# A gated delta-rule attention with a softplus MLP on one core: the first pair of chunks inverted chunk by chunk, and a new order of all items

## The chip, the cores and the metric

The kernel runs on one core of one Trainium2 chip, as one program. Time is device microseconds (us) of that core; three runs of the kernel before gave 239.97, 241.2 and 242.23, median 241.2. A profile of one further execution goes with it.

## The reference

Four batches of eight heads, 768 time steps, head size 48. A linear-attention state of 48 by 48 per head is read and updated at each step, and the gated result goes through an MLP with softplus (3072 tokens, 384 to 2048 to 384):

```python
k_n = k / (np.linalg.norm(k, axis=-1, keepdims=True) + 1e-06)
for t in range(S):
    kt, vt, bt = (k_n[:, :, t].copy(), v[:, :, t].copy(), beta[:, :, t, None].copy())
    readout = np.einsum('bhd,bhde->bhe', q[:, :, t], state)
    y[:, :, t] = g[:, :, t] * readout
    v_old = np.einsum('bhde,bhd->bhe', state, kt)
    state = state + bt[:, :, :, None] * np.einsum('bhd,bhe->bhde', kt, vt - v_old)
...
x = np.ascontiguousarray(attn_out.transpose(0, 2, 1, 3)).reshape(B * S, H * D)
h = x @ w_in
g = np.maximum(h, 0.0) + np.log1p(np.exp(-np.abs(h)))
return (g @ w_out).astype(np.float32)
```

## The kernel before, in words

**Chunks.** The 768 steps are cut into 12 chunks of 64. Within a chunk the recurrence is solved at once: with G the products of the chunk's keys with each other, the effect of the steps on each other is the inverse of a 64 by 64 lower triangular matrix for each of 32 heads. Only the state then passes from chunk to chunk. Each chunk goes through four kinds of work.

- *Loads and norms* (`norms`, `front`): k, q, v and g of a chunk come in as two DMAs of 192 KB each, all issued by SyncE (SP) but for a few. The keys are squared (`ksq`, L348 to L350), summed over 48 (`red`, L359), and the root is taken (`sqrt` on ScalarE, ACT, for chunks 0 to 3, `pow` on GpSimd, POOL, after that) with `eps` behind it. Keys and queries are cast or scaled to fp16 (`cast`, `kmul`), transposed on TensorE (PE; `trs`, L419 and L451) and copied out of PSUM (`kev`, `qev`).
- *Products* (`gram`, L513): keys with keys, and keys with queries. The first are copied out negated (`kkc`, into the tile kk), the second are masked by VectorE, DVE (`mask`, L495). For chunks 0 and 1 (`N_SPLIT = 2`) both are separate items of 64 columns; later chunks have one item of 128. For chunks 0 and 1 there is also `gramd` (L537), which gives the 32 by 32 diagonal blocks alone, copied out as `kd`.
- *Inverse* (`inverse`), for a pair of chunks at a time (`GROUPS`): the 16 by 16 diagonal blocks are brought into lanes by a DVE transpose (`ln`, L594 or L601), scaled by beta (`prep`, L641), and inverted by 15 steps that depend on each other (`step`, L653 to L668; step j is a product into tmp and a sum into tt of 2(15-j)(j+1) elements, on DVE or POOL). The result is masked into three buffers (`ca`, `cb`, L683 and L685) and transposed back (`st`, L711, three for a pair). Two rounds of small matmuls (`xmm` L741, `tmm` L771, then `zmm` L792, with `xs`, `td2` and `z` copying out of PSUM) build the 64 by 64 inverse from its blocks.
- *Chain* (`chain`), one chunk after the other: `ks` and `qs` (L829) apply the old state, `w` (L869) subtracts, `umm` (L883) and `zu` (L896) apply the inverse with copies `u1` and `u2`, `smm` (L913) and `s` (L927) make the new state, `ymm` (L939), `y` (L953), `ytr` (L966) and `xt` give the chunk's gated output, transposed. For chunk 0 there is no old state, and `w0` (L861) scales v.
- *Dense*: `g1` (L992, six matmuls of 256 columns or three of 512 twice), softplus on ACT (`soft`, L1004), `g2` (L1019, four matmuls of 384 columns) and `o`, then a store. Chunks 0, 1, 10 and 11 have dense jobs of their own (16 items of g1 and g2 each), 2 to 9 go in pairs (32 items). The weights come in eight quarters by DMAs that POOL issues (`wload`, L327).

**Order.** Nothing is scheduled by rule: `emit` runs one table (`_ORDER`) of some 1260 words such as `D227`, an engine's letter (P, D, A, G for POOL, S for SyncE) and an item's number. So each engine's queue has one fixed order, and an instruction that waits holds back all behind it on its engine. `fill` items (L1049) are matmuls on the identity whose result nobody reads; the table has twelve of them, four matmuls each.

**beta for chunks 0 and 1** comes by four DMAs that POOL issues ahead of its first work (L179), into lanes laid out for the pair; the rest of beta by eight DMAs on SP (L262).

Of the kernel before, what the change touches and what calls it, by code (L numbers as in the profile page):

```python
# [87 lines left out]
def kernel(  # L88
# [474 lines left out]

    def inverse(gi):
# [8 lines left out]
        if RAW[c0]:  # L573
            nl, bl, nv = Buf(r_nl), Buf(r_bl), nv_of[c0]

            def lbeta(en):
                nc.vector.transpose(nl.ap, nv.ap)
                nc.vector.reciprocal(nl.ap, nl.ap)
                nc.vector.tensor_tensor(bl.ap, beta_l[:, gi], nl.ap, ALU.mult)
                nc.vector.tensor_tensor(bl.ap, bl.ap, nl.ap, ALU.mult)  # L580

            bl_it = [add("lbeta", tag, "D", lbeta, deps=[nv_it[c] for c in cs], bufs=[nv, nl, bl])]
            blb, bl_of = [bl], lambda: bl.ap
        else:
            bl_it, blb, bl_of = [], [], lambda: beta_l[:, gi]
# [4 lines left out]
        def lnt(en):  # L590
            o = words(ln.ap.rearrange("p w s e -> p (w s e)"))[:, : nw * HC]
            if compact:
                i = words(kd_of[gi].ap.rearrange("p c u t -> p (c u t)"))
                nc.vector.transpose(  # L594
                    o.rearrange("p (w n) -> p w n", w=nw),
                    i.rearrange("p (n w) -> p w n", w=nw),
                )
                return
# [132 lines left out]
        def uv(ap):  # L731
            return ap.rearrange("p (u c) -> p u c", c=HC)

        for cl, c in enumerate(cs):
            xp, ep, xs = [Buf(p_d), Buf(p_d)], [Buf(p_d), Buf(p_d)], Buf(r_xs)

            def xmm(en, cl=cl, xp=xp):
                for n in range(H):
                    for p in range(2):
                        for r in range(2):  # L740
                            nc.tensor.matmul(  # L741
                                uv(xp[p].ap)[HALF[r ^ p], n],
                                kk.ap[HALF[r], cl, H * p + n, HC:],
                                dn.ap[HALF[r], cl, H * p + n],
                            )

            e3 = add("xmm", f"{c}", "P", xmm, deps=[ta_it] + kk_it[c], bufs=[kk, dn] + xp, mm=32,
                     mode="64")
            def pickx(en, xp, xs, p):
                o = xs.ap[:, H * p : H * p + H].rearrange("p u (x b j) -> p u x b j", x=2, b=2)  # L750
                i = uv(xp[p].ap)[:, :H].rearrange("p u (x j) -> p u x j", x=2)
                if en == "D":
                    nc.vector.tensor_tensor(
                        o[:, :, :, 0], i, mk[:, None, :, None].broadcast_to([P, H, 2, 16]),
                        ALU.mult)
                    return
                for x in range(2):
                    nc.scalar.activation(
                        o[:, :, x, 0], i[:, :, x], AF.Copy, scale=mk[:, x : x + 1])

            e4 = [add("xs", f"{c}.{p}", "DA",
                      lambda en, xp=xp, xs=xs, p=p: pickx(en, xp, xs, p),
                      deps=[e3], bufs=[xp[p], xs], size=256)
                  for p in range(2)]

            def tmm(en, cl=cl, ep=ep, xs=xs):
                for n in range(H):
                    for p in range(2):
                        for r in range(2):
                            h = HALF[r ^ p]  # L770
                            nc.tensor.matmul(  # L771
                                uv(ep[p].ap)[HALF[r], n],
                                xs.ap[h, H * p + n],
                                tx.ap[h, cl, n] if p else tb.ap[h, cl, n],
                            )

            e5 = add("tmm", f"{c}", "P", tmm, deps=e4 + [tb_it] + tx_it, bufs=[xs, tb, tx] + ep,
                     mm=32, mode="64")
            td2 = [add("td2", f"{c}.{p}", "AD",
                       lambda en, cl=cl, ep=ep, p=p: copy(  # L780
                           en,
                           td.ap[:, cl, H * p : H * p + H]
                           .rearrange("p u (k b j) -> p u k b j", k=3, b=2)[:, :, 1:, 1],
                           uv(ep[p].ap)[:, :H].rearrange("p u (x j) -> p u x j", x=2)),
                       deps=[e5], bufs=[ep[p], td], size=256)
                   for p in range(2)]
            zp, z = [Buf(p_d), Buf(p_d)], Buf(r_z)

            def zmm(en, cl=cl, zp=zp):
                for r, p, i, m in CROSS:  # L790
                    u = H * p + 2 * i + m
                    nc.tensor.matmul(  # L792
                        zp[r].ap.rearrange("p (n c) -> p n c", c=64)[HALF[r ^ p], 2 * i + m, :HC],
                        kk.ap[HALF[r], cl, u, : 2 * HC],
                        td.ap[HALF[r], cl, u, 2 * HC :],
                    )

            z1 = add("zmm", f"{c}", "P", zmm, deps=td2 + [td_it], bufs=[kk, td] + zp, mm=32,
                     mode="64")
            z_it = []  # L800
            for r in range(2):
                z_it.append(
                    add("z", f"{c}.{r}", "AD",
                        lambda en, r=r, z=z, zp=zp: copy(
                            en, z.ap[:, r, :, HC:],
                            zp[r].ap.rearrange("p (n c) -> p n c", c=64)[:, :, :HC]),
                        deps=[z1], bufs=[zp[r], z], size=256))
            td_of[c] = td
            z_of[c] = (z, z_it, [td_it] + td2)
# [356 lines left out]
```

## Time and profile before

| | |
|---|---|
| runs | 239.97, 241.2, 242.23 us |
| profiled execution | 240.57 us, of which the span of its instructions is 238.9 us |
| busy | PE 217.7, DVE 170.6, ACT 146.8, POOL 114.7 us |
| loaded and stored | 27.57 MB, 115 GB/s over the span |
| mean granted clock of PE | 0.941 |

An engine's busy time is the union of its instructions' times. The windows view gives it by stretch, with the clock that PE was granted (1.00 is full) and the share of the DMA engines' time. A row of the timeline has the start, the duration, the engine, the line, the operation, output and inputs, and how many such follow each other; in square brackets stands how long the engine was idle before it and what ended that.

### The profile page before, as it was taken

Reading aid. Unit: us, or ns where it says so; the run is one execution under the profiler, and the core shown is the slowest. Engines: PE = TensorE matmul, PEld = TensorE weight load, DVE = VectorE, ACT = ScalarE, POOL = GpSimd, SP = SyncE. Lnnn points to the kernel's source line nnn. Section 1 sums busy time; section 2 is a strip of 40 time slices with the busy share of each in tenths; the row PEclk is TensorE's granted clock in tenths of the full one; section 3 lists DMA queues with packets and bytes.
Section 4 is the critical chain, followed back from the end, with each engine's and each line's share of the span. In section 5 each row is a group of like instructions: output and inputs, shape, how many; then the busy total and the mean of one; then the engine's idle time right before and its main releaser. Section 6 shows DMA issues by size and latency. Waiting matters only on the chain.

```text
span 238.9 us, 11420 instructions
## 1 busy us (share of the span) xinstructions
PE 217.7 (91%) x5016; PEld 141.2 (59%) x5016; DVE 170.6 (71%) x374; ACT 146.8 (61%) x293; POOL 114.7 (48%) x203
## 2 busy tenths in 40 slices
PE   7768568899998799999999999999999999999993
PEld 2345357678564575556665567645667456678761
DVE  7689898956988958799787997596774784742010
ACT  4569789489777435974469745698614674053710
POOL 8815465984763962438787788830027220000000
PEclk9997955599999958999999999999999999999999
DMA  7999999999876799578698343592103430200023
GB/s 100 201 210 152 204 130 157 178 187 199 145 144 137 175 180 149 119 136 139 152 164 162 75 79 63 135 139 48 21 20 71 82 69 21 68 22 16 19 53 95
DMA packets 86833, 27.57 MB, mean 115 GB/s; under 512 B 77048, under 2 KB 86776, under 8 KB 86784
## 3 DMA queue, kind: packets, MB, share of 16 engines
q1 hardware_dynamic: 81360, 21.72, 52.3%
q0 software_dynamic: 3840, 3.17, 8.8%
q10 hardware_dynamic: 1584, 1.97, 3.4%
q8 instruction: 39, 0.64, 1.2%
q14 instruction: 10, 0.08, 0.1%
HBM read 25.26 MB, written 4.72 MB: 126 GB/s over the span
## 4 chain that ended last, share of the span: by engine, by line
PE 72%; POOL 8%; DVE 6%; ACT 5%; issue 4%; DMA 3%; SPq 1%; DVEq 0%; POOLq 0%; ACTq 0%
PE d L992 26%; PE d L1019 22%; PE d L513 3%; PE d L939 3%; DMA f<-in_k_dram 3%; POOL tt L668 3%; PE d L829 2%; PE d L451 2%; POOL tmp L661 2%; PE d L419 2%; PE d L1049 2%; PE d L966 2%; PE d L883 2%; PE d L792 2%; DVE mt L495 2%
## 5 line engine op out<-in xcount | busy, mean ns | idle before, releaser
L1019 PE MATMUL d<-w_out,ga 128*128 128x384 f16 x384 | 70.0, 327 | 0.0
L992 PE MATMUL d<-xt,w_in 128*128 128x512 f16 (+1 forms) x384 | 69.0, 330 | 0.0
L1004 ACT ACTIVATE ga<-d 128x512 f16<-128x512 f32 x96 | 52.8, 604 | 12.7 <-PE d L992 10.8
L992 PEld LDWEIGHTS <-w_in 128*128 128x128 f16 x384 | 35.9, 99 | 22.2 <-issue 0.3
L1019 PEld LDWEIGHTS <-ga 128*128 128x128 f16 x384 | 34.9, 98 | 22.0 <-issue 1.1
L661 POOL TENSOR_TENSOR tmp<-nn,tt 128x78 f32<-128x78 f32 (+7 forms) x58 | 20.6, 356 | 16.3 <-DVE tt L668 12.5
L370 POOL TENSOR_TENSOR nv<-nv,half_c 128x16 f32<-128x16 f32 x8 | 23.5, 2933 | 9.1 <-DVE nv L359 9.0
L668 POOL TENSOR_TENSOR tt<-tt,tmp 128x78 f32<-128x78 f32 (+7 forms) x58 | 22.6, 390 | 4.5
L207 ACT ACTIVATE kqt<-d 128x1024 f16<-128x1024 f16 x18 | 18.3, 1023 | 9.1 <-PE d L451 7.6
L495 DVE TENSOR_TENSOR mt<-d,mask 128x256 f16<-128x256 f32 x48 | 19.0, 414 | 3.3 <-PE d L513 2.9
L207 ACT ACTIVATE osb<-d 128x384 f32<-128x384 f32 x15 | 7.3, 489 | 21.9 <-PE d L1019 21.8
L207 ACT ACTIVATE u<-d 128x384 f16<-128x384 f32 x29 | 13.5, 492 | 11.7 <-PE d L896 5.9
L641 POOL TENSOR_TENSOR nn<-ln,beta_l 128x256 f32<-128x256 f16 x9 | 7.5, 854 | 23.1 <-DVE ln L624 23.0
L953 DVE TENSOR_TENSOR yg<-d,f 128x384 f16<-128x384 f32 x24 | 12.7, 547 | 5.9 <-PE d L939 4.1
L1049 PE MATMUL d<-ident 128*128 128x512 f16 x48 | 14.9, 459 | 1.7 <-DVE ident L195 1.7
L209 DVE CAST u<-d 128x384 f16<-128x384 f32 x19 | 10.2, 552 | 7.3 <-PE d L896 4.0
L209 DVE COPY osb<-d 128x384 f32<-128x384 f32 x9 | 5.0, 552 | 14.0 <-PE d L1019 14.0
L513 PE MATMUL d<-kqt 48*64 48x128 f16 (+1 forms) x448 | 11.6, 229 | 2.8 <-ACT kqt L207 1.3
L869 DVE TENSOR_TENSOR w<-f,d 128x384 f16<-128x384 f32 x22 | 11.3, 539 | 3.1 <-PE d L829 2.7
L927 DVE TENSOR_TENSOR s<-s,d 128x384 f16<-128x384 f16 x20 | 10.7, 547 | 3.0 <-PE d L913 2.9
L209 POOL COPY tx<-tb 64x512 f16<-64x512 f16 x8 | 4.9, 607 | 16.1 <-DVE tb L711 7.4
L359 DVE TENSOR_REDUCE nv<-f 128x16 f32<-128x768 f32 x12 | 11.3, 941 | 1.4 <-POOL f L350 1.4
(117 smaller groups left out, 368.9 us busy)
## 6 DMA issues: line engine op xcount, KB each, us to landing
f<-in_k_dram SPq DMA_DIRECT2D x24, 192.0 KB, 6.0
f<-in_v_dram SPq DMA_DIRECT2D x24, 192.0 KB, 5.8
f<-in_g_dram SPq DMA_DIRECT2D x24, 192.0 KB, 4.4
f<-in_q_dram SPq DMA_DIRECT2D x23, 192.0 KB, 4.7
out_dram<-osb SPq DMA_DIRECT2D x30, 96.0 KB, 2.3
out_dram<-osb ACTq DMA_DIRECT2D x18, 96.0 KB, 2.4
w_in<-in_moe_w_in_dram POOLq DMA_DIRECT2D x4, 384.0 KB, 6.7
w_out<-in_moe_w_out_dram POOLq DMA_DIRECT2D x4, 384.0 KB, 9.9
```

Of the source, the lines that this page charges most:

```text
L207: nc.scalar.activation(o, x, AF.Copy, scale=float(sign))
L209: ENG[en].tensor_copy(o, x)
L370: nc.gpsimd.tensor_tensor(nvs(), nvs(), half_c[:, :NU], ALU.pow)
L495: nc.vector.tensor_tensor(mt[c][m].ap[:, NP * p : NP * p + NP], gb[m].ap.rearrange("p (i b) -> p i b", i=NP)[:, :, n : n + C], mask[:, Non ...
L513: nc.tensor.matmul(gb[m].ap.rearrange("p (i b) -> p i b", i=NP)[HALF[r], i, lo:hi], x[:, :C], x[:, lo:hi],)
L661: ENG[en].tensor_tensor(t, nn.ap[:, :, j : j + 1, j + 1 :].broadcast_to([P, 2, w, n]), tt.ap[:, :, :w, j : j + 1].broadcast_to([P, 2, w, n ...
L668: ENG[en].tensor_tensor(rows, rows, t, ALU.add)
L953: lambda en, m=m: nc.vector.tensor_tensor(heads(yg.ap, m), hd(yp[m].ap), heads(gf.ap, m), ALU.mult),
L992: nc.tensor.matmul(hp.ap[:, n * b : n * b + n], w_in[:, j, f * P : (f + 1) * P], xt.ap[:, j, t0 : t0 + n], start=(j == 0), stop=(j == 2),)
L1004: lambda en, hp=hp, o=gb: nc.scalar.activation(o.ap, hp.ap, AF.Softplus),
L1019: nc.tensor.matmul(op.ap[:, :DM], b.ap[:, col + c0 : col + c0 + 128], w_out[:, f, :], start=(f == 0), stop=(f == NF - 1),)
L1049: nc.tensor.matmul(hp.ap, ident, ident[:, None, :].broadcast_to([P, 4, P]))
```

## The change

Chunks 0 and 1 are no longer inverted as a pair. A new function `solo` does for one chunk what `inverse` does for two: half the elements in each step, one transpose `ln1` of 256 words (before, one of 512 for the pair), a selection `pick1` since the 32 by 32 blocks of one chunk fill the lanes in another way, and two transposes back (`st`) for each chunk, where the pair had three. The norms for it come by five small DVE instructions (`lbeta`), once for each chunk; before, four for both. What stood at the end of `inverse` is moved into a function `join` and called from both. The tile t1 of `solo` takes the ring of tb.

```diff
-N_SPLIT = 2
+N_SPLIT = 0
...
-N_FILL = 40
+N_FILL = 80
...
-    for r in range(2):
-        for x in range(2):
-            l0 = 32 * (2 * r + x)
-            bt = beta[2 * r : 2 * r + 2].rearrange("p h (c l) -> c (p h) l", l=C)
-            nc.gpsimd.dma_start(
-                out=beta_l[l0 : l0 + 32, 0], in_=bt[:2, :, HC * x : HC * x + HC]
-            )
...
-                beta_it.append(add("bload", f"{r}{x}{a}", "S", bload))
+                beta_it.append(add("bload", f"{r}{x}{a}", "SA", bload))
...
+                    ENG[en].dma_start(
+                        out=beta_s[l0 : l0 + 32, c],
+                        in_=bt[c, :, HC * x : HC * x + HC].rearrange("u (b k) -> b u k", b=2),
+                    )
+
+                lone_it[c].append(add("bload", f"s{r}{x}{c}", "SA", lone))
...
+        def lbeta(en):
+            nc.vector.transpose(
+                nl.ap.rearrange("p (b u) -> p b u", b=2),
+                nv.ap[:, NU * cl : NU * cl + NU][:, None, :].broadcast_to([P, 2, NU]),
+            )
+            n = nl.ap[:, :16]
+            nc.vector.copy_predicated(
+                words(n), odd.broadcast_to([P, 16]), words(nl.ap[:, 16:]))
+            nc.vector.reciprocal(n, n)
+            nc.vector.tensor_tensor(bl.ap[:, :16], beta_s[:, cl], n, ALU.mult)
+            nc.vector.tensor_tensor(bl.ap[:, :16], bl.ap[:, :16], n, ALU.mult)
...
+        def step(en, j):
+            n, w = 15 - j, j + 1
...
+            t = tmp.ap[:, : n * w].rearrange("p (c i) -> p c i", c=w)
+            ENG[en].tensor_tensor(
+                t,
+                nn.ap[:, 0, j : j + 1, j + 1 :].broadcast_to([P, w, n]),
+                tt.ap[:, 0, :w, j : j + 1].broadcast_to([P, w, n]),
+                ALU.mult,
+            )
+            rows = tt.ap[:, 0, :w, j + 1 :]
+            ENG[en].tensor_tensor(rows, rows, t, ALU.add)
...
+        def both(en, x):
+            for b, m in enumerate((mz, mk)):
+                masked(en, rows()[:, 16 * b : 16 * b + 16, x], tt.ap[:, 0], m[:, x : x + 1])
...
+        ta_it = add("st", f"{tag}.a", "D", lambda en: lanes_out(dn.ap, ta.ap, 0, 1),
+                    deps=ca, bufs=[ta, dn], size=512)
+        td_it = add("st", f"{tag}.b", "D", lambda en: lanes_out(td.ap, rows(), 2, 2),
+                    deps=cb, bufs=[t1, td], size=512)
...
         def fill(en, hp=hp):
-            for _ in range(4):
+            for _ in range(2):
                 nc.tensor.matmul(hp.ap, ident, ident[:, None, :].broadcast_to([P, 4, P]))
...
+        if gi in DIAGONALS:
+            for cl, c in enumerate(cs):
+                solo(c, cl, kk_of[gi])
+            return
...
-S25 S26 D227 S34 S33 D6 D11 A176 D173 A9 A1 G169 D170 D0 A171 G5 A197 A12 P129 P152 P164 P132 P162
+S34 S33 D16 D3 P180 P200 P148 P156 P183 D221 A25 A13 A9 A28 S30 A217 D218 P182 S42 S41 S27 S26 G224
```

The new table has 19 fills of two matmuls, 38 in all where 48 stood before. The moves that matter below, as the queues stand:

On DVE, from the transpose into lanes to the first steps, before (tt and tmp are the tiles of the 15 steps, kk the negated products, td the inverse under construction):

```order
L594 STREAM_TRANSPOSE ln_112<-dn_121 128x512
L641 TENSOR_TENSOR nn_113<-ln_112,bl_96 128x256 x2
L211 TENSOR_SCALAR kk_97<-d_169 128x4x64
L661 TENSOR_TENSOR tmp_115<-nn_113,tt_117 128x56
L668 TENSOR_TENSOR tt_117<-tt_117,tmp_115 128x2x2x14
```

and the same place now, for chunk 0 alone:

```order
L681 STREAM_TRANSPOSE ln_115<-kd_125 128x256
L691 COPY_PREDICATED ln_115<-mb,ln_115 128x8x16
L702 TENSOR_TENSOR nn_116<-ln_115,bl_99 128x256
L245 MEMSET qn_94 128x16x8
L208 COPY kqt_104<-d_175 128x4x2x64
L373 TENSOR_REDUCE nv_95<-f_82 128x16
L208 COPY td_130<-pat 128x16x32
L208 COPY kqt_104<-d_177 128x4x2x64
L208 COPY td_129<-pat 128x16x32
L718 TENSOR_TENSOR tmp_118<-nn_116,tt_120 128x60
L725 TENSOR_TENSOR tt_120<-tt_120,tmp_118 128x6x10
```

DVE now takes chunk 0's steps 5 to 9 and 14, POOL 0 to 4 and 10 to 13; the evictions of chunk 1's keys and its sum of squares stand ahead of step 5.

On DVE, around the two multiplications by the gate of chunk 0 (yg, item `y`), before:

```order
L211 TENSOR_SCALAR kk_98<-d_168 128x4x64
L953 TENSOR_TENSOR yg_145<-d_171,f_75 128x8x48
L495 TENSOR_TENSOR mt_111<-d_168,mask 128x256
L953 TENSOR_TENSOR yg_145<-d_174,f_75 128x8x48
L601 STREAM_TRANSPOSE ln_112<-kk_98 128x1024
```

and now (ta, tb and td are the masked steps of chunk 1 and what they are transposed into):

```order
L737 TENSOR_SCALAR tb_126<-tt_121,mz 128x16x16
L737 TENSOR_SCALAR tb_126<-tt_121,mk 128x16x16
L1078 TENSOR_TENSOR yg_149<-d_178,f_88 128x8x48
L1078 TENSOR_TENSOR yg_149<-d_172,f_88 128x8x48
L757 STREAM_TRANSPOSE td_130<-tb_126 128x2x8x32
L737 TENSOR_SCALAR ta_123<-tt_121,mz 128x16x16
L509 TENSOR_TENSOR mt_113<-d_172,mask 128x256
L757 STREAM_TRANSPOSE dn_124<-ta_123 128x16x32
```

Chunk 1's transposes back now stand behind chunk 0's gate, and PE has `xmm` of chunk 1, which reads the last of them, ahead of its first g1; before, both chunks' `xmm` were long past. The transpose into lanes for chunks 2 and 3 follows five instructions later.

On POOL, the DMAs of w_out (the second weight), before:

```order
L327 DMA w_out<-in_moe_w_out_dram 128x4x384 x3
L641 TENSOR_TENSOR nn_114<-ln_112,beta_l 128x256 x2
L653 TENSOR_TENSOR tt_118<-nn_114,tt_118 128x2x15
```

and now:

```order
L208 COPY tx_127<-td_130 64x256
L341 DMA w_out<-in_moe_w_out_dram 128x4x384
L970 TENSOR_TENSOR f_81<-f_81,nv_95 128x768
L833 MEMSET tt_120 128x512
L341 DMA w_out<-in_moe_w_out_dram 128x4x384
L208 COPY tx_127<-td_130 64x256
L835 COPY tt_120<-beta_l 128x2x16
L842 TENSOR_TENSOR nn_116<-ln_115,beta_l 128x256 x2
L854 TENSOR_TENSOR tt_120<-nn_116,tt_120 128x2x15
L341 DMA w_out<-in_moe_w_out_dram 128x4x384
```

Three quarters of w_out were issued together, ahead of the inverse of chunks 2 and 3; now the second quarter (the third of these DMAs) stands behind that inverse's `prep` (nn) and its step 0, and the last quarter behind step 1 and a `pow`.

More of the change, by code (lines that the diff above doesn't have):

```diff
@@ L134 @@
     mx = pool.tile([P, 2], F32, name="mx")
+    mz = pool.tile([P, 2], F32, name="mz")
+    mb = pool.tile([P, 1], F32, name="mb")
+    beta_s = pool.tile([P, 2, 16], F32, name="beta_s")
     beta_l = pool.tile([P, len(GROUPS), HC], F32, name="beta_l")
@@ L265, in bload, with lone @@
                     )
-                beta_it.append(add("bload", f"{r}{x}{a}", "S", bload))
+                beta_it.append(add("bload", f"{r}{x}{a}", "SA", bload))
+    lone_it = [[], []]
+    for c in range(2):
+        for r in range(2):
+            for x in range(2):
+                def lone(en, r=r, x=x, c=c):
+                    l0 = 32 * (2 * r + x)
+                    bt = beta[2 * r : 2 * r + 2].rearrange("p h (c l) -> c (p h) l", l=C)
+                    ENG[en].dma_start(
[3 more added lines that the diff above has]
+                lone_it[c].append(add("bload", f"s{r}{x}{c}", "SA", lone))
     def f16ps(ap):
@@ L572, in inverse @@
         en0 = INV_ENG[gi]
[L573 to L585, printed above, removed]
+        bl_it, blb, bl_of = [], [], lambda: beta_l[:, gi]
         ln, nn, tt, tmp = Buf(r_ln), Buf(r_n), Buf(r_t), Buf(r_tmp)
-        compact = gi in DIAGONALS
-        nw = 32 if pair and not compact else 16
+        nw = 32 if pair else 16
         def lnt(en):
             o = words(ln.ap.rearrange("p w s e -> p (w s e)"))[:, : nw * HC]
[L592 to L598, printed above, removed]
             i = words(kk.ap.rearrange("p c u t -> p (c u t)"))
@@ L609, in lnt @@
                 )
-        l1 = add("ln", tag, "D", lnt, deps=kd_it[gi] if compact else kdeps,
-                 bufs=[kd_of[gi] if compact else kk, ln], size=nw * HC)
-        if pair and not compact:
+        l1 = add("ln", tag, "D", lnt, deps=kdeps, bufs=[kk, ln], size=nw * HC)
+        if pair:
             def pick(en):
@@ L729, in inverse @@
             for r in range(2)]
-        def uv(ap):
-            return ap.rearrange("p (u c) -> p u c", c=HC)
         for cl, c in enumerate(cs):
[L735 to L809, printed above, removed]
@@ L811 @@
+            join(c, cl, cl, kk, dn, tx, td, ta_it, tb_it, td_it, tx_it, tb,
+                 lambda h, n, cl=cl: tb.ap[h, cl, n])
     state = [None, []]
@@ L1047, in fill @@
         def fill(en, hp=hp):
-            for _ in range(4):
+            for _ in range(2):
                 nc.tensor.matmul(hp.ap, ident, ident[:, None, :].broadcast_to([P, 4, P]))
-        add("fill", f"{n}", "P", fill, bufs=[hp], mm=4, mode="full", size=512)
+        add("fill", f"{n}", "P", fill, bufs=[hp], mm=2, mode="full", size=512)
     for gi, cs in enumerate(GROUPS):
@@ L1136 @@
+S1326 S1356 S1350
 """
```

296 lines of the change are left out of this document (223 added, 73 removed).

## The prediction

> **What bounds the kernel now.** I read the windows view first, in stretches of 20 us, to see which engine has no room left, and where.
>
> ```profile
> core 0: us, PE busy (x) PEld busy (x) DVE busy (x) ACT busy (x) POOL busy (x), PEclk, DMA share, GB/s
> 0.00:20.00 20.00, 13.87 (x252) 7.06 (x253) 15.91 (x46) 11.33 (x22) 11.96 (x29) 0.99 1.04 170
> 20.00:40.00 20.00, 14.93 (x435) 11.54 (x435) 17.46 (x44) 17.21 (x35) 10.49 (x18) 0.67 1.05 164
> 40.00:60.00 20.00, 18.09 (x409) 15.00 (x406) 14.33 (x35) 15.07 (x28) 15.42 (x28) 0.83 1.17 181
> 60.00:80.00 20.00, 18.02 (x538) 11.35 (x537) 18.00 (x36) 13.52 (x28) 12.11 (x17) 1.00 0.76 141
> 80.00:100.00 20.00, 18.21 (x330) 11.53 (x328) 15.86 (x33) 12.50 (x25) 11.16 (x18) 0.83 1.00 169
> 100.00:120.00 20.00, 19.97 (x608) 12.55 (x608) 16.78 (x34) 12.26 (x27) 13.19 (x24) 1.00 0.70 133
> 200.00:220.00 20.00, 20.00 (x489) 14.66 (x477) 10.51 (x22) 5.16 (x10) 0.00 (x0) 1.00 0.17 38
> ```
>
> From 100 us on PE is full at a full clock, and the end is PE's work added up. Before that it is not: the first row counts fills, the second has a clock of 0.67. There DVE is the fullest engine, with 17.46 and 18.00 of 20 us in two rows. Then I looked in the timeline for the points that later work hangs on.
>
> ```profile
> 6.38 0.37 DVE L209 CAST kn<-f 128x384 f16<-128x384 f32 x1 [0.23 <-DMA f<-in_k_dram]
> ...
> 16.16 0.24 POOL L653 TENSOR_TENSOR tt<-nn,tt 128x30 f32<-128x30 f32 x1 [1.79 <-DVE nn L641]
> ...
> 27.83 0.26 POOL L668 TENSOR_TENSOR tt<-tt,tmp 128x30 f32<-128x30 f32 x1
> ...
> 37.41 0.74 PE L896 MATMUL d<-u,z 64*64 64x48 f16 x32
> ...
> 41.84 0.55 DVE L953 TENSOR_TENSOR yg<-d,f 128x384 f16<-128x384 f32 x1
> ...
> 44.18 1.46 PE L992 MATMUL d<-xt,w_in 128*128 128x256 f16 x6
> ...
> 78.45 0.43 PE L829 MATMUL d<-s,kqt 48*64 48x48 f16 x31 [0.31 <-DVE yg L953]
> ...
> 91.02 1.31 PE L992 MATMUL d<-xt,w_in 128*128 128x512 f16 x5
> ...
> 226.99 7.96 PE L1019 MATMUL d<-w_out,ga 128*128 128x384 f16 x48
> ```
>
> Keys land at 6.4; the pair's 15 steps run from 16.16 to 28.09; chunk 0's zu starts at 37.41, its gate ends at 42.39, the first g1 comes at 44.18. At 91.02 comes the first g1 of chunks 2 and 3 together. From there PE runs to 234.95 and a store ends the span at 238.9: 147.9 us, which I take as fixed, since the new table leaves PE the same there (160 dense items, eight chunks' chains; it has one gram more behind it and one smm less). So **the question is when chunks 2 and 3 reach their g1**, now 91.02.
>
> **The change, part by part.** Prices:
>
> ```profile
> L661 POOL TENSOR_TENSOR tmp<-nn,tt x58: 250/354/576, 18.8 to 188.5; 128x78 f32<-128x78 f32 x11, 128x96 f32<-128x96 f32 x9, 128x56 f32<-128x56 f32 x9, 128x120 f32<-128x120 f32 x8
> L661 DVE TENSOR_TENSOR tmp<-nn,tt x26: 213/280/293, 16.4 to 189.8; 128x126 f32<-128x126 f32 x6, 128x110 f32<-128x110 f32 x4, 128x128 f32<-128x128 f32 x4, 128x120 f32<-128x120 f32 x4
> ...
> 14.18 1.04 DVE L594 STREAM_TRANSPOSE ln<-dn 128x512 uint32<-128x512 uint32 x1
> 13.27 0.35 DVE L578 RECIPROCAL nl<-nl 128x32 f32<-128x32 f32 x1
> 9.39 0.84 ACT L348 ACTIVATE f<-f 128x768 f32<-128x768 f32 x1
> 5.88 0.27 DVE L209 COPY td<-pat 128x512 f16<-128x512 f16 x1
> 27.59 1.40 DVE L495 TENSOR_TENSOR mt<-d,mask 128x256 f16<-128x256 f32 x4
> ...
> L359 DVE TENSOR_REDUCE nv<-f 128x16 f32<-128x768 f32 x12 | 11.3, 941 | 1.4 <-POOL f L350 1.4
> L601 DVE STREAM_TRANSPOSE ln<-kk 128x1024 uint32<-128x1024 uint32 x5 | 9.7, 1932 | 0.5 <-ACT kk L207 0.4
> L711 DVE STREAM_TRANSPOSE dn<-ta 128x512 uint32<-128x512 uint32 x6 | 6.4, 1060 | 0.2
> ```
>
> A step that depends on the one before costs its time plus some 0.04 us on DVE and 0.08 on POOL: 0.25 and 0.33 for the halved sizes. The four masks in 1.40 show that independent instructions overlap: 0.35 each.
>
> *To the first step.* The squares of chunk 0 move from POOL to ACT (0.84), the sum on DVE (0.94) ends at 8.2; eviction, eps, two fixed copies (0.27 each) bring DVE to 9.3. Then lbeta, five dependent ones of 0.2 to 0.35, 1.3 us; ln1 of half the words, 0.55; pick1 0.3; prep 0.4. lbeta needs four of the small beta DMAs, the last issued by SP as the seventh, near 6.
>
> ```profile
> beta_l<-in_beta_dram SPq DMA_DIRECT2D x8, 10.0 KB, 6.3
> beta_l<-in_beta_dram POOLq DMA_DIRECT2D x4, 4.0 KB, 4.8
> ```
>
> With 4.3 us, a little under the smaller median because the second key chunk ahead of it takes its time either way, it is there at 10.3 (bounds: at 9.3 it costs nothing; at 12.3, by the 6.3, two more us). First step at 10.3 + 1.3 + 0.55 + 0.3 + 0.4 = 12.9: **3.3 earlier**.
>
> *The 15 steps of chunk 0.* POOL 9 instructions (3.0), DVE 10 (2.5), POOL 8 (2.6), DVE 2 (0.5), hand-overs 0.4. DVE has seven other items before its last step, 3.2 us against POOL's 2.6: 0.6 more. 9.6 in all, end at 22.5 where 28.09 stood: **5.6 earlier**.
>
> *From there to zu.* Here it is lost again. DVE is in order, and ahead of chunk 0's last z stand ten instructions of 256 elements (4.1), two transposes (2.1), two sums (1.9), four of 384 (2.2), two of 768 (1.6), three steps of chunk 1 (1.3) and seven short ones (1.8): 15.0, or 14.5 with the overlap. zu at 37.0: **0.4 earlier**. Moving w0 and kmul of chunk 3 here from POOL and doing part of chunk 1's steps has used up the rest.
>
> *First g1.* From zu to the gate's end now takes 42.39 - 37.41 = 5.0: 42.0. Behind it DVE does two transposes back for chunk 1, a ca and a mask, 2.1 + 0.7: 44.8. PE's xmm of chunk 1 waits for them, 0.5, and only then comes the first g1: 45.3, **1.1 later**.
>
> *To the g1 of chunks 2 and 3.* DVE from 44.8 to the new state of chunk 2: 30 instructions of 256 (12.3), twelve of 384 (6.6), three transposes (3.2), two of 1024 words (3.9), four sums (3.8), two kmul (2.0), a key eviction (0.7), nine steps of two (5.0), four short (1.0): 38.5, with overlap 37.4, so 82.2. From ks of chunk 3 to the g1 took 91.02 - 78.45 = 12.6, with the inverse of chunk 3 still being put together; without that the instructions alone are 7.6. I take 8, near the lower, because the new table has zmm of chunk 3 long done: 90.2.
>
> On top come waits of DVE itself. It was idle 5.7 and 2.0 us in 40:60 and 60:80; so 0 to 8 us. One source I can name:
>
> ```profile
> 44.55 2.28 POOL L327 DMA_DIRECT2D w_out<-in_moe_w_out_dram  x3
> 46.81 2.17 POOL L641 TENSOR_TENSOR nn<-ln,beta_l 128x256 f32<-128x256 f16 x2
> ...
> 59.66 1.46 PE L1019 MATMUL d<-w_out,ga 128*128 128x384 f16 x8
> ...
> DMA to landing us min/median/max: 8.4/9.9/13.2
> ```
>
> Three quarters of w_out were issued from 44.55, and the first g2 came at 59.66. Now the first quarter is issued behind a tx that reads chunk 1's transpose, near 43.3, landing at 53.2; PE has its first g2 behind umm of chunk 1, near 51. The second quarter stands behind nn (2.17, from about 49) and step 0: issued near 52, landing at 62, and wanted near 59. That is some 4.5 us of waiting on PE. PE's own work from 45.3 to that g1 I count as 39.3 (32 dense items of 0.66 by 7.96 / 12, the rest chains and grams); with 4.5 it is 43.8, still under DVE's 44.9, so most is hidden. But behind the waiting g2 stand the transposes and grams of chunk 4, whose masks DVE meets in order. Of 0 to 4.5 I let 1.6 through: 91.8, **0.8 later**.
>
> *Products merged, fills, beta off POOL.* Merging the products saves 64 matmuls on PE before 40 us, where PE waits for DVE anyway: nothing; without that cover it would give 0.9 us, by the 31 in 0.43 us of the row at 78.45. Ten fewer fill matmuls: the clock in 20:40 was 0.67 with them; nothing. POOL's four beta DMAs went ahead of work that waits for keys: nothing.
>
> *Contention of DVE and POOL.* POOL's 40 step instructions of the two chunks run next to DVE.
>
> ```profile
> 51.38 0.39 POOL L668 TENSOR_TENSOR tt<-tt,tmp 128x96 f32<-128x96 f32 x1
> 143.57 1.12 DVE L403 TENSOR_TENSOR kn<-f,nv 128x768 f16<-128x768 f32 x1
> 143.95 0.99 POOL L668 TENSOR_TENSOR tt<-tt,tmp 128x96 f32<-128x96 f32 x1
> ```
>
> The same step took 0.99 in place of 0.39 when a kmul ran on DVE. The Trainium skill's page "SBUF — State Buffer", section "Who interferes with whom", says that a VectorE instruction with two SBUF inputs locks out a GpSimd instruction that reads SBUF; by that rule, these rows agree. I put 0 into the sum, since few such instructions fall there, and keep it as a rival.
>
> **Sum.** 238.9 + 0.8 = 239.7 of span; 1.7 around it (240.57 - 238.9): 241.4 for that execution, which lies 0.6 under the median: **242.0**.
>
> **Rivals.**
>
> *Faster: the clock holds.* In the stretch before the g1 of chunks 2 and 3, PE starved and its clock fell.
>
> ```profile
> 84.00:88.00 4.00, 3.47 (x49) 2.46 (x48) 2.33 (x5) 1.02 (x4) 2.71 (x7) 0.54 1.08 165
> 88.00:92.00 4.00, 4.00 (x73) 3.12 (x72) 2.48 (x5) 1.25 (x3) 1.10 (x4) 0.60 1.15 165
> ```
>
> That lost 4 x 0.46 + 4 x 0.40 = 3.4 us. The new table keeps g2 of chunk 1 for this stretch. If the weights land in time as well, g1 comes at 90.2 - 3.4 = 86.8, the span is 234.7, the median 237.0. For it: the g2 items between; against it: DVE's sum, which no clock shortens.
>
> *Slower: w_out is late.* The same quarters at the longest landing, 13.2, come 3.3 us later each; two of them make PE's sum 39.3 + 4.5 + 6.6 = 50.4, over DVE's 44.9: g1 at 95.7, span 243.6, 246.5. It decides from landings of about 10.5 us on (4.5 + 2 x 0.6). For it: a DMA share of 1.17 in 40:60, and the second quarter's place behind nn; against it: the median of 9.9.
>
> *Slower: POOL locked out.* Chunk 1's steps on POOL meet w0 twice and kmul of chunk 3, those of chunk 2 the next kmul: four times 0.6 to 0.7, so 2.5 us on the way to xmm: 244.5. For it the 0.99; against it that w0 has half the elements.
>
> **How the numbers follow.** Near 242, within 239 to 244, is the likeliest: 0.36. The faster rival 0.30, late weights 0.28, the lock 0.06. A measurement of this kernel tells about 1% from no change, 238.8 to 243.6. So faster 0.30, same 0.36, slower 0.34. The range, 235 to 248, takes in both rivals, two us under the one (a DVE that waits less than its sum) and the late weights with one us more.
>
> **What would show it.** Right: chunk 0's steps begin near 13 and end near 22.5; zu of chunk 0 near 37; the first g1 near 45 with xmm of chunk 1 just ahead; DVE over 90% busy from 45 to 80; g2 waiting for DMA near 51 and 60; the g1 of chunks 2 and 3 near 92; 147.9 us from there. Wrong: a first g1 before 42, which would mean that DVE's items overlap more than I count; a first g1 of chunks 2 and 3 before 89; or PE idle after it.

## The result, and the profile of the changed kernel

The changed kernel takes 242.37 us (median of 20 runs, 240.42 to 244.16), the kernel before beside it 240.70 (20 runs, 237.12 to 245.0). The ratio is 1.0152, with a 95% interval of 1.0122 to 1.0181: **slower by 1.5%**. It is taken over fast runs alone, those at most 1.5% above the fastest of the same kernel, and the runs of the kernel before scatter more, so that the medians of all twenty lie only 0.7% apart. The forecast was 242.0 in a range of 235 to 248, and the number held. "Within 1%" was put at 0.36 and "slower by over 1%" at 0.34: by the forecast's own bounds (238.8 to 243.6) the first came true, by the ratio the second, so the two chances say little here.

The profiled execution took 244.16 us (span 242.4), the longest of the 20 and 1.8 over their median. What only this one execution shows is therefore held against the experiments below. The points that the prediction named, in the timeline of the changed kernel (start, duration, engine, line, operation, count, and in brackets the idle time before it and what ended it):

```profile
12.31 0.21 POOL L713 TENSOR_TENSOR tt<-nn,tt 128x15 f32<-128x15 f32 x1 [1.14 <-DVE qn L245]
...
22.21 0.18 DVE L725 TENSOR_TENSOR tt<-tt,tmp 128x15 f32<-128x15 f32 x1
...
36.91 0.44 PE L1021 MATMUL d<-u,z 64*64 64x48 f16 x32
...
39.72 1.02 DVE L1078 TENSOR_TENSOR yg<-d,f 128x384 f16<-128x384 f32 x2
...
43.60 0.43 PE L586 MATMUL d<-dn,kk 64*64 64x32 f16 x32 [0.99 <-DVE dn L757]
43.96 2.14 PE L1117 MATMUL d<-xt,w_in 128*128 128x256 f16 x18
...
50.56 0.21 PE L637 MATMUL d<-td,kk 64*64 64x32 f16 x3 [1.87 <-issue]
53.05 1.44 PE L1144 MATMUL d<-w_out,ga 128*128 128x384 f16 x4 [2.02 <-DMA w_out<-in_moe_w_out_dram]
...
62.16 0.55 DVE L1052 TENSOR_TENSOR s<-s,d 128x384 f16<-128x384 f16 x1 [4.02 <-PE d L1038]
63.09 1.02 DVE L1078 TENSOR_TENSOR yg<-d,f 128x384 f16<-128x384 f32 x2
...
84.99 1.01 DVE L1052 TENSOR_TENSOR s<-s,d 128x384 f16<-128x384 f16 x2
...
94.38 2.77 PE L1117 MATMUL d<-xt,w_in 128*128 128x512 f16 x12
```

Chunk 0's steps begin at 12.31 and end at 22.39, its zu comes at 36.91, its gate ends at 40.74, the first g1 comes at 43.96, the first g1 of chunks 2 and 3 at 94.38. PE stands twice around 50 us, the second time for the weight w_out; behind that DVE waits 4.02 us for PE.

Cutting both executions at the two g1 (windows view) tells where the time went. First the kernel before, then the changed one:

```profile
core 0: us, PE busy (x) PEld busy (x) DVE busy (x) ACT busy (x) POOL busy (x), PEclk, DMA share, GB/s
0.00:44.18 44.18, 31.63 (x795) 20.95 (x795) 37.55 (x97) 31.66 (x61) 26.46 (x50) 0.80 1.01 165
44.18:91.02 46.84, 42.51 (x1054) 31.09 (x1046) 35.78 (x80) 29.97 (x59) 31.18 (x54) 0.90 0.99 167
91.02:238.90 147.88, 143.52 (x3180) 89.19 (x3176) 97.31 (x200) 85.14 (x174) 57.01 (x100) 1.00 0.45 84
```

```profile
0.00:43.96 43.96, 26.76 (x616) 15.61 (x617) 36.19 (x105) 29.12 (x61) 26.46 (x71) 0.81 1.07 164
43.96:94.38 50.42, 43.28 (x1145) 31.39 (x1135) 42.23 (x94) 32.10 (x62) 34.53 (x53) 0.93 0.97 166
94.38:242.40 148.02, 143.48 (x3192) 89.36 (x3192) 96.92 (x209) 86.57 (x177) 54.27 (x89) 1.00 0.43 81
```

The first stretch is 0.22 us shorter, the last 0.14 longer. The 3.5 us of this execution lie in the middle one: 50.42 in place of 46.84. There DVE has 14 instructions and 6.45 us of work more (42.23 against 35.78); in the first stretch it has 1.36 less. Together DVE does 5.1 us more before the g1 of chunks 2 and 3 (78.42 against 73.33). The view by line names most of it. For chunks 0 and 1, DVE's transposes into lanes, the selection, the norms and the transposes back took 5.2 us for the pair (1.04, none, 0.95 and 3.24) and take 8.1 apart (1.22, 0.60, 1.97 and 4.28): 2.8 us are the price of inverting two chunks apart. The rest is what the new table moved to DVE, such as the two w0 (1.2 us, before on POOL) and five more casts of z (2.1 us, before on ACT), less what it took away. PE was no less full than DVE in this stretch: 42.51 us before and 43.28 now. PE's clock in the middle is a little better than before (0.93 against 0.90).

### The profile page after: what moved, and what is told of

It is laid out like the page before. It is cut to its first block, busy times and chain, and to the rows that moved or that the text cites. A ratio compares the mean times of both kernels' runs of the same rounds, so it can differ in the third digit from the quotient of the medians.

```text
span 242.4 us, 11307 instructions
## 1 busy us (share of the span) xinstructions
PE 213.5 (88%) x4942; PEld 136.4 (56%) x4942; DVE 175.3 (72%) x406; ACT 147.8 (61%) x300; POOL 115.3 (48%) x211
## 4 chain that ended last, share of the span: by engine, by line
PE 63%; DVE 13%; POOL 8%; DMA 6%; ACT 3%; issue 3%; SPq 1%; ACTq 1%; POOLq 0%; DVEq 0%
PE d L1144 24%; PE d L1117 21%; DMA w_out<-in_moe_w_out_dram 4%; PE d L954 2%; PE d L1064 2%; DMA f<-in_v_dram 2%; PE d L1174 2%; POOL tmp L862 2%; PE d L527 2%; POOL tt L869 2%; PE d L433 1%; POOL tt L725 1%; PE d L1091 1%; POOL tmp L718 1%; PE d L1038 1%
## 5 line engine op out<-in xcount | busy, mean ns | idle before, releaser
L1144 PE MATMUL d<-w_out,ga 128*128 128x384 f16 x384 | 71.1, 331 | 2.1 <-DMA w_out<-in_moe_w_out_dram 2.0
L1129 ACT ACTIVATE ga<-d 128x512 f16<-128x512 f32 x96 | 54.1, 603 | 19.5 <-PE d L1117 18.6
L1117 PEld LDWEIGHTS <-w_in 128*128 128x128 f16 x384 | 36.5, 99 | 24.5 <-issue 1.4
L862 POOL TENSOR_TENSOR tmp<-nn,tt 128x110 f32<-128x110 f32 (+7 forms) x44 | 16.2, 369 | 18.9 <-DVE tt L869 16.2
L206 ACT ACTIVATE kqt<-d 128x1024 f16<-128x1024 f16 (+1 forms) x18 | 17.8, 1001 | 6.3 <-PE d L433 4.0
L869 POOL TENSOR_TENSOR tt<-tt,tmp 128x110 f32<-128x110 f32 (+7 forms) x44 | 17.6, 400 | 3.5
L465 PE MATMUL d<-ident,qn 128*128 128x128 f16 x96 | 8.7, 243 | 8.7 <-DVE qn L208 8.4
L842 POOL TENSOR_TENSOR nn<-ln,beta_l 128x256 f32<-128x256 f16 x5 | 3.8, 774 | 25.0 <-DVE ln L825 25.0
L206 ACT ACTIVATE kk<-d 128x256 f16<-128x256 f32 x29 | 10.7, 385 | 5.4 <-DVE mt L509 2.7
L527 PE MATMUL d<-kqt 48*64 48x128 f16 x384 | 9.9, 227 | 2.7 <-ACT kqt L206 1.8
```

Source lines behind the costliest of these rows:

```text
L206: nc.scalar.activation(o, x, AF.Copy, scale=float(sign))
L527: nc.tensor.matmul(gb[m].ap.rearrange("p (i b) -> p i b", i=NP)[HALF[r], i, lo:hi], x[:, :C], x[:, lo:hi],)
L862: ENG[en].tensor_tensor(t, nn.ap[:, :, j : j + 1, j + 1 :].broadcast_to([P, 2, w, n]), tt.ap[:, :, :w, j : j + 1].broadcast_to([P, 2, w, n ...
L869: ENG[en].tensor_tensor(rows, rows, t, ALU.add)
L1117: nc.tensor.matmul(hp.ap[:, n * b : n * b + n], w_in[:, j, f * P : (f + 1) * P], xt.ap[:, j, t0 : t0 + n], start=(j == 0), stop=(j == 2),)
L1129: lambda en, hp=hp, o=gb: nc.scalar.activation(o.ap, hp.ap, AF.Softplus),
```

## The experiments

They test these explanations. **A**: the late first quarter of w_out stops PE, and the clock falls. **B**: DVE's queue sets the time up to the g1 of chunks 2 and 3. **P**: at the first g1, PE still owes ks, tmm and zmm of chunk 1 and a trs of chunk 4, which the old order had behind it. **L**: several transfers are late, one behind the other. **D**: the merge alone matters. Each ratio is to the kernel before on the same chip, with its 95% interval; the changed kernel stands at 1.0152. All but the two on the split (e4 and m1) and the two with added sums (y1 and y2) change only the table of the order (item names as in the code).

**Weights early (e1).** POOL:

```diff
 wload:w0.1
+wload:w1.0 wload:w1.1 wload:w1.2 wload:w1.3
 tx:1.0
-wload:w1.0 (and the other three from their places behind vs, step 2.0 and pow)
```

> The four quarters of w_out are issued on POOL right behind the last of w_in (near 39.7 us) and not from 42.35 on. Theory A (the late weight): the first g2 of chunk 0 no longer waits for its weight, it runs near 51 where it ran at 53.05, the clock does not fall to half in 52 to 59, and the first g1 of chunks 2 and 3 comes 2.5 to 4 us before 94.4; time 238.5 to 240, ratio to the kernel before 0.99 to 1.00. Theory B (DVE's longer list sets that g1): first g2 earlier all the same, but the g1 of chunks 2 and 3 stays within 0.7 us of 94.4 and the time at 242, ratio 1.01 to 1.02.

Measured: 242.21 us, ratio 1.0102 [1.0055, 1.015]. The timeline of this kernel:

```profile
50.57 0.82 PE L1144 MATMUL d<-w_out,ga 128*128 128x384 f16 x4
...
56.55 0.49 PE L1117 MATMUL d<-xt,w_in 128*128 128x256 f16 x3 [1.20 <-issue]
...
60.52 1.02 DVE L1078 TENSOR_TENSOR yg<-d,f 128x384 f16<-128x384 f32 x2 [0.80 <-DMA f<-in_k_dram]
...
81.55 1.01 DVE L1052 TENSOR_TENSOR s<-s,d 128x384 f16<-128x384 f16 x2
...
92.91 4.71 PE L1117 MATMUL d<-xt,w_in 128*128 128x512 f16 x21
```

The wait is gone, g2 runs at 50.57. Yet the time is not 2.4 to 3.9 us lower, as A asked; against 1.0152 the gain is 0.5% with an uncertainty of about as much. The time is as B put it; B's place for the g1, within 0.7 us of 94.4, is missed by the 92.91, but 94.38 is from an execution 1.8 us over its median. The new state of chunk 2 is ready at 82.56 where it was 86.00, but then 10.35 us pass to the g1 in place of 8.38.

**g2 behind the g1 (e2).** PE:

```diff
 umm:1
-g2:0.1.0
 qs:1 zu:1
-g2:0.0.0
 g1:0.8 g1:0.14 g1:0.4 g1:0.10
+g2:0.1.0 g2:0.0.0
 ymm:1
```

> The weights stay late; the two g2 items that wait for them stand behind the four g1 on PE. Theory A: qs and zu of chunk 1 and the g1 no longer stand behind the wait; zu of chunk 1 near 51.5 in place of 54.86, the clock does not fall to half, and the g1 of chunks 2 and 3 comes 2 to 4 us before 94.4; time 238.5 to 240.5. Theory B: zu earlier, g1 of chunks 2 and 3 within 0.7 us of 94.4, time 242.

Measured: 242.82 us, ratio 1.0119 [1.0063, 1.0174]. In its trace the g1 of chunks 2 and 3 comes at 91.94, 2.4 us before the other profile, but over six runs the gain is no larger than that of e1.

**Fills (e3).** PE, three unused fill items:

```diff
 umm:1
+fill fill fill
 g2:0.1.0
```

> Six fill matmuls of 512 columns stand ahead of the waiting g2; the wait for the weight stays, the time on PE is filled. Theory A with the clock as its larger part: the clock stays near full in 53 to 60, the 24 matmuls of the four g1 take about 2.6 us in place of 3.83, and the g1 of chunks 2 and 3 comes 1.5 to 2 us earlier; time near 240.5. Theory A with the wait itself as its larger part, or theory B: within 0.7 us of 242.4.

Measured: 242.36 us, ratio 1.0111 [1.0062, 1.016]. No gain that can be told from none. But the run doesn't test the clock: its low stretch came at 40 to 48 us here, ahead of the fills, which had nothing left to save. That stretch doesn't stay in place; two windows views, the changed kernel first, then e1:

```profile
40.00:48.00 8.00, 6.63 (x163) 4.63 (x162) 7.83 (x15) 7.05 (x17) 4.94 (x8) 1.00 1.28 193
...
52.00:60.00 8.00, 6.96 (x94) 4.53 (x94) 5.59 (x18) 2.33 (x6) 4.21 (x5) 0.58 1.29 198
```

```profile
40.00:48.00 8.00, 7.40 (x109) 4.69 (x108) 6.56 (x11) 5.09 (x12) 5.13 (x9) 0.57 1.24 189
...
52.00:60.00 8.00, 6.57 (x144) 5.04 (x137) 6.42 (x20) 5.24 (x10) 3.97 (x5) 1.00 1.25 213
```

One low stretch comes in either, between 52 and 60 or between 40 and 48. So the half clock behind the late weight, which looked like its consequence, comes without that wait too, only earlier.

**Products split (e4).** `N_SPLIT = 2`; each `gram` of chunks 0 and 1 becomes a `gramk` at its place and a `gramq` ahead of the first mask that reads it.

> The products of keys and queries of chunks 0 and 1 are two items again, 64 more matmuls of PE before 30 us. By the prediction this costs nothing, since PE waits for DVE there: 242.4, within 0.7. Rival D (the merge is worth its matmuls): 0.9 us longer, 243.3. That the merge itself delays DVE, because evictions of the keys' products now wait for queries: shorter by up to 1 us.

Measured: 245.68 us, ratio 1.0248 [1.0194, 1.0302]: 1% or 2.3 us over the changed kernel. The windows 30 to 40 us, the split first, then the changed kernel:

```profile
30.00:40.00 10.00, 9.48 (x237) 6.25 (x236) 8.04 (x24) 5.11 (x12) 7.84 (x18) 0.56 1.01 144
```

```profile
30.00:40.00 10.00, 8.66 (x265) 5.66 (x258) 8.87 (x25) 6.66 (x15) 8.02 (x18) 0.76 0.98 149
```

At 0.56 of the clock PE has no room there (9.48 of 10 us): in this profile the cover under which the merge was costed at nothing does not exist. The first g1 came at 45.79, 1.8 us later. None of the three answers was near 245.68, and the cover doesn't explain all of it: from the g1 of chunks 2 and 3 (95.23) to the end of the span (244.5) this execution takes 149.3 us, where the changed kernel takes 148.0.

**Half an order with half of the other (h1, h2).** h1: the changed kernel's table up to umm of chunk 1, all later items as the table before has them. h2: the reverse.

> The changed kernel up to umm of chunk 1 (near 50 us); all later items in the order of the kernel before. Theory P (the loss is made before 50 us: at the first g1 the new order still owes ks, tmm and zmm of chunk 1 and a trs of chunk 4, which PE had behind it before; 1.7 us by their rows): the time stays near 242.4, ratio 1.005 to 1.02. Rival (the new order of the later items costs it): 240.5, ratio 0.995 to 1.005.

> The kernel before up to the same place (diag of chunk 4), all later items in the order of the changed kernel. Theory P: the time is that of the kernel before, 240.5 or a little less, ratio 0.99 to 1.00. Rival (the new order of the later items costs it): 242 to 243, ratio over 1.005.

Measured: 247.13 us, ratio 1.0314 [1.0261, 1.0368], and 246.19 us, 1.0275 [1.0212, 1.0337]. Both are slower than either whole; neither answer was foreseen, and they don't say which half costs. In h2, for example, PE stood 4.10 us for w_in, since the old first half issues that quarter later than the new second half wants it. An order does not come apart into halves.

**Weights and gate early (x1), transfers by need (x5).** Both with e1:

```diff
 ACT: load:g1.0
+load:g1.1
 ... soft:0.2
-load:g1.1
 SP, x5 alone:
-load:g2.1 load:q7.1 load:q8.1 (from their places among the weights)
 load:k7.0
+load:g2.1 load:q7.1 load:q8.1
```

> w_out early as in the first experiment, and the second half of chunk 1's gate issued right behind its first half (near 42 us in place of 48.9), since y of chunk 1 waited on DVE until 60.5 once the weight was early. Theory L (late transfers, one behind the other): y of chunk 1 near 58.5, DVE's queue behind it 1 to 2 us earlier, the g1 of chunks 2 and 3 near 91, time 240.5 to 241.5. Theory P: 242, within 0.7.

> As x1, and three halves of g of chunk 2 and q of chunks 7 and 8, wanted 20 us later or more, are issued behind k of chunk 7 and not among the weights. Theory L: transfers between 40 and 62 land sooner than 10 us from issue, time 240 to 241. Theory P: 242, within 0.7.

Measured: 242.53 us, ratio 1.0112 [1.005, 1.0174], and 242.03 us, 1.0101 [1.0045, 1.0157]. L's forecast falls, but L itself is not refuted, since the transfer that was to come early did not: y of chunk 1 still came at 60.95 in x1, though the gate's second half was issued at 42.50 where it was 48.89 in e1. The profile lets a load of keys end that wait; but ACT's queue, with nothing but the gate on it, moved its last six packets in the same microsecond, 60 to 61, and in x5 the profile lets a load of g end the same wait (61.05). The view of the DMA queues says why. One microsecond of x1, then 46 to 60 us (queue, kind, packets, MB, share of 16 engines; q0 is POOL's with the weights, q1 SP's; q10, which carried 0.39 MB here, the size of the gate's two halves, is ACT's):

```profile
q0 software_dynamic: 167, 0.12, 77.9%
q1 hardware_dynamic: 165, 0.03, 28.7%
q10 hardware_dynamic: 166, 0.03, 16.1%
```

```profile
q0 software_dynamic: 2015, 1.50, 68.2%
q1 hardware_dynamic: 3322, 0.97, 43.7%
q10 hardware_dynamic: 2074, 0.39, 14.5%
```

The three queues are served packet for packet as long as each has work: from 52 to 54 us they move 325, 325 and 322 packets. The 3322 of q1 come from the end of the stretch, when the weights are nearly through and q1 moves 1408 in two microseconds (58 to 60). A packet of the weights carries four times as much as one of the gate, so the gate crawls at 0.03 MB a microsecond until w_out is through. Half of its 2074 packets keep ACT's queue busy until about 52.5, so it made no difference that the second was issued earlier. Weights that come earlier let y of chunk 1 wait instead of g2.

**DVE relieved (d1).** Engines of eight items:

```diff
-D fix:2.kk20  D tx:0.0 tx:0.1  D z:0.1 z:0.0  D u1:0.1 u2:0.0  D ca:1.0
+G fix:2.kk20  A tx:0.0 tx:0.1  A z:0.1 z:0.0  A u1:0.1 u2:0.0  A ca:1.0
```

> Eight short items of DVE between 26 and 42 us go to engines that stand idle there (two tx, two z, a u and the last u of chunk 0 and a ca of chunk 1 to ACT, a fixed copy of 0.80 us for chunk 2 to POOL): 2.6 us less on DVE ahead of the last z of chunk 0, 3.5 us ahead of the first g1. Theory B (DVE's queue sets the first 45 us): zu of chunk 0 2 us earlier, near 35; first g1 near 42; time 1 to 2 us less, 240.5 to 241.5. Rival (the chains of chunk 1 through POOL's steps and PE set it): first g1 within 0.7 us of 44 and the time within 0.7 of 242.4.

Measured: 246.42 us, ratio 1.0307 [1.0251, 1.0364]. My relief was a burden. In the timeline of d1:

```profile
38.25 0.44 PE L1021 MATMUL d<-u,z 64*64 64x48 f16 x32 [0.92 <-ACT z L206]
...
44.98 0.75 ACT L735 ACTIVATE ta<-tt,mz 128x256 f16<-128x256 f32 x1
45.76 1.06 DVE L757 STREAM_TRANSPOSE dn<-ta 128x512 uint32<-128x512 uint32 x1 [1.93 <-ACT ta L735]
...
46.87 0.43 PE L586 MATMUL d<-dn,kk 64*64 64x32 f16 x32 [3.01 <-DVE dn L757]
```

The last z and the ca now stand behind evictions on ACT that wait for PE; DVE, with time to spare, waits 1.93 us for ACT, and xmm of chunk 1 comes 3.3 us later than before the move (46.87 against 43.60). The run doesn't tell B from its rival, since it moved the wait and not only the work. What it does show: 3.3 us at the first g1 go with 3.7 us at the end (0.0155 x 239). That is no rule: in x5 the first g1 comes 1.1 us late (45.06) at no loss.

**DVE loaded (y1, y2).** Two useless sums, at two places of DVE's queue:

```diff
+    mb3 = mask[:, None, :].broadcast_to([P, 12, C])
+    for i in range(2):
+        add("extra", f"{i}", "D", lambda en: nc.vector.tensor_reduce(
+            dmy, mb3, axis=mybir.AxisListType.X, op=ALU.add))
 y1: ahead of u1:0.0        y2: ahead of w:2.0
```

> Two useless sums of 768 elements (0.9 us each by the row of the sums) are put on DVE right ahead of the first u of chunk 0, near 34 us. Theory B: everything behind is 1.8 us later and so is the end: 244.2, within 0.7. Rival: less than half of it comes through, 242.4 to 243.2.

> The same two useless sums (1.88 us together) stand on DVE right ahead of w of chunk 2, near 72 us, where DVE was 98% busy. If DVE's queue sets the g1 of chunks 2 and 3, as the prediction's longest term has it: that g1 and the end 1.9 us later, ratio to the kernel before near 1.023. If from the first g1 on the list of PE sets it (theory P), and DVE has slack to give: 0.6 us or less, ratio 1.013 to 1.018.

Measured: y1 245.45 us, ratio 1.0284 [1.0241, 1.0326]; y2 245.38 us, 1.0225 [1.0181, 1.0269]. In y1 the sums, the first g1 and the first g1 of chunks 2 and 3:

```profile
34.87 1.88 DVE L1194 TENSOR_REDUCE dmy<-mask 128x12 f32<-128x768 f16 x2
...
42.96 1.02 DVE L1079 TENSOR_TENSOR yg<-d,f 128x384 f16<-128x384 f32 x2 [1.57 <-PE d L1065]
...
47.20 2.14 PE L1118 MATMUL d<-xt,w_in 128*128 128x256 f16 x18
...
95.86 2.76 PE L1118 MATMUL d<-xt,w_in 128*128 128x512 f16 x12
```

and in y2 (an execution of 247.18 us, the longest of its six, so that the verdict rests on the ratio and the place of the g1 is a hint):

```profile
72.37 1.94 DVE L1194 TENSOR_REDUCE dmy<-mask 128x12 f32<-128x768 f16 x2
...
88.17 1.01 DVE L1053 TENSOR_TENSOR s<-s,d 128x384 f16<-128x384 f16 x2
...
97.41 2.76 PE L1118 MATMUL d<-xt,w_in 128*128 128x512 f16 x12
```

Over the changed kernel's 1.0152, 1.88 us of DVE near 35 us cost 1.3% or 3.2 us, and 1.94 us near 72 cost 0.73% or 1.75 us. DVE's time comes through at both places: at least whole near 35 and, within what the runs can tell, about whole near 72. So DVE has no slack there, as B says. The number for y2 is B's; P's upper end (1.018) lies just at the edge of its interval. The number for y1 is above B's own (1.8 within 0.7), and its profile shows where more may come from: PE stands 2.11 us for DVE behind the sums, its clock is 0.52 from 36 to 43 us, and DVE waits 1.57 us for the products behind the gate, which take 1.03 us where they took 0.67. One engine's delay is passed on by the other.

**The merge alone (m1).** The kernel before with `N_SPLIT = 0`, `gram` at the place of `gramq`; the evictions of the keys' products follow it. (The split that its expectation speaks of is e4.)

> The kernel before with one part of the change: the products of keys and queries of chunks 0 and 1 are merged (at the place of the queries' products, the evictions of the keys' products behind them); all else in the old order. By the prediction: no change, 240.5 within 0.7. Rival (as the fifth run of the split suggests, 3.3 us): 238 to 239.5. Rival (evictions that now wait for queries hold up DVE): 241.5 or more.

Measured: 243.07 us, ratio 1.0199 [1.0155, 1.0244]. In the old order the merge goes with a loss of 2%, the size that the third guess had; in the new one it saves 1%. It has no price of its own. The guess's reason is not shown: in the profile of m1 the g1 of chunks 2 and 3 comes at 91.07, as before (91.02), and 149.7 us follow where 147.9 did.

No version beat the kernel before.

## Why the prediction came out as it did

**The start was right.** Its points were 12.9, 22.5 and 37.0 for the first step, the last step and zu; measured 12.31, 22.39 and 36.91. The gain at the steps' end, 5.7 us, was lost again in DVE's queue, as forecast: from there to zu are 14.52 us, put at 14.5, and DVE is busy for 13.76 of them. Gate and first g1 came 1.3 us sooner than put (40.74 for 42.0, 43.96 for 45.3): the step "from zu to the gate's end now takes 5.0" was taken over from the kernel before, and is 3.8 in the changed one.

**DVE's sum was the right question and 1.8 us too long.** 37.4 was put for DVE's work from the end of chunk 1's transposes to the new state of chunk 2. Between those points (43.55 and 86.00) the windows view has:

```profile
43.55:86.00 42.45, 35.70 (x924) 25.76 (x924) 35.58 (x77) 28.02 (x56) 29.60 (x39) 0.92 0.96 169
86.00:94.38 8.38, 7.95 (x243) 5.97 (x242) 7.06 (x19) 4.39 (x7) 5.34 (x14) 1.00 1.02 151
```

and in e1:

```profile
43.53:82.56 39.03, 34.26 (x919) 25.15 (x919) 35.51 (x77) 28.26 (x56) 26.54 (x36) 0.96 1.10 185
82.56:92.91 10.35, 8.73 (x247) 6.27 (x247) 7.00 (x19) 4.39 (x7) 7.00 (x19) 1.00 1.09 159
```

35.5 us of work, and 3.5 to 6.9 us of waits in place of the 1.6 that I let through. "DVE over 90% busy from 45 to 80" is not so in the profiled execution (28.16 of 35 us, 80%) and just about so in e1 (31.48, 90%), where PE is as busy (31.25). The last step, "I take 8", is 8.38 and 10.35.

**That the total held is luck in part.** In e1 the sum comes out as 1.3 us sooner at the transposes, 1.9 less work, 1.9 more waits and 2.4 more in the last step, which makes 92.91 of 91.8. In the profiled execution the waits alone are 5.3 us longer than put. The errors have different signs, and nothing in the prediction said that they would cancel.

**The weight was placed right and its worth was not.** The first g2 waited until 53.05, as put (53.2). The second wait, near 60, did not come, since PE was late itself. The step that failed is "most is hidden ... I let 1.6 through": DVE waited 3.5 us even where the weight was early. In the five tries without the wait the ratio is 1.0101 to 1.0119 against 1.0152, a gain of 0.8 to 1.2 us, and each interval overlaps that of the changed kernel. The two that leave the weight as late as it was (e2 and e3) gain as much as the three that bring it early, so the gain can't be put down to the weight. In e1 and x1 the same bytes then hold up the gate. The slower rival, "w_out is late", named the right transfer and the wrong reason for the loss. (Its time was also added up wrongly: a span of 243.6 gives 245.9, not 246.5.)

**The clock did hold**, as the faster rival has it: 0.54 and 0.60 before the g1 of chunks 2 and 3 became 1.00 (the row from 86.00). Yet the g1 did not come sooner. The rival held "DVE's sum, which no clock shortens" against itself; with 5.1 us more of DVE's work ahead of that g1 and DVE without slack near 72 us (y2), that sentence fits best, though no run tests it.

**The lock came too, but smaller.** On POOL two steps of chunk 1 beside w0 took 0.50 and 0.72 us where 0.30 is usual (31.23 and 31.81), and one of chunk 2 beside kmul took 1.00 where 0.40 is usual (57.40): 1.2 us in all, between the 0 of the sum and the 2.5 of the rival. No run shows how much of it reaches the g1.

**Products merged at nothing** was wrong. The step reads "PE waits for DVE anyway" from the mean of 20 us; at the lower clock of e4 it does not, and the split costs 2.3 us, not 0.9. The two other terms put at nothing, the fills left out and beta's DMAs off POOL, were not tried alone.

**The rest of the sum.** 147.9 us from the g1 of chunks 2 and 3 were 148.0, and 147.2 to 148.2 in e1, e2 and y1. By the median, that g1 stands near 242.37 - 1.76 - 148.0 = 92.6. The 91.8 was put for an execution 0.6 us under the median, so it stands for 92.4.

**What made it slower** is, as far as the runs go, the 5.1 us of DVE work more ahead of that g1, of which waits that got shorter give some back. This is argued, not shown. y1 and y2 show that DVE's time counts at two places. That taking work off DVE would give it back is not shown: d1 put it in the wrong place. P isn't refuted on its own; it describes the same delay by PE's list. And the prediction's "DVE is the fullest engine" holds only for the first 40 us: from 40 to 100 its own rows have PE as full or fuller (18.09, 18.02 and 18.21 of 20 us, against 14.33, 18.00 and 15.86).

## What to carry to other kernels

Where two engines pass a chain to and fro, count each engine's work up to the point that later work hangs on, before and after (78.4 against 73.3 us here): a gain in a chain's latency (5.7 us at the steps) that is paid for with work of an engine without slack can be lost again. A wait removed from one queue is worth what the next wait leaves of it, so look up what lands next on the same DMA engines before moving a weight up. To price an engine's time at a place, add a useless instruction there; to move work off it says more about the place it went to.

## What the hardware showed that was not expected

- *Queues share by packets, not by bytes.* 167, 165 and 166 packets in one microsecond carried 0.12, 0.03 and 0.03 MB (x1, above). The Trainium skill's page "DMA: Bandwidth & Descriptors", section "Queues, rings and completion order", says that an engine goes round its queues packet by packet; by that rule, these rows agree.
- *PE stops now and then where a block of 256 of its instructions ends.* In d1 two stops in the middle of equal matmuls, with nothing that ends them:

```profile
54.55 0.21 PE L637 MATMUL d<-td,kk 64*64 64x32 f16 x3 [1.26 <-issue]
...
61.57 0.71 PE L1117 MATMUL d<-xt,w_in 128*128 128x256 f16 x3 [1.97 <-issue]
```

```profile
54.55:61.57 7.02, 5.05 (x128) 3.79 (x128) 5.93 (x20) 4.48 (x9) 4.52 (x5) 1.00 1.32 200
```

  Between them lie 128 matmuls and 128 weight loads. The 1.87 us at 50.56 in the changed kernel and the 1.20 at 56.55 in e1 are of the same kind. The page "Runtime: NRT & Kernel Launch" of the Trainium skill, section "Instruction fetch mechanics", has programs arrive in blocks of 256 instructions and calls the cost mostly hidden; at these four stops it cost 1.2 to 2.0 us each. That the block was late can be read from the DMA records. They have a queue q8, of kind instruction, with 38 packets of 16 KB. At the stops that end at 54.55 and 61.57 in d1, at 50.56 in the changed kernel and at 56.55 in e1, such a packet starts 2.2 to 2.7 us and lands 1.3 to 1.5 us before PE goes on, and the other stops of this kind in the first 100 us of the traces agree (1.2 to 1.8 us).
- *A short DVE step takes two to four times as long beside POOL.* In d1, with a cast and a copy on POOL:

```profile
28.20 0.81 DVE L718 TENSOR_TENSOR tmp<-nn,tt 128x60 f32<-128x60 f32 x1 [0.20 <-POOL tt L725]
...
29.04 0.52 DVE L725 TENSOR_TENSOR tt<-tt,tmp 128x60 f32<-128x60 f32 x1
```

  The same two took 0.20 and 0.22 in the changed kernel, where POOL stood idle. Each ends within 0.1 us of POOL's instruction (the cast at 28.93, the copy at 29.50). The lock that I held against POOL alone works both ways.
